# Output stores of the first ten token blocks issued from GpSimd's queue and not from SyncE's, in an attention and gated-FFN kernel

## Chip, cores and metric

The kernel runs on one core of one Trainium2 chip. The metric is the device time of one execution in microseconds (us); lower is better. The time of a version is the median of several executions.

The engines are called as the profile calls them: PE is TensorE (matrix products), PEld its weight loads, DVE is VectorE, ACT is ScalarE, POOL is GpSimd, SP is SyncE. SP computes nothing here; it issues DMAs. SPq and POOLq are the instruction queues of SP and POOL: an engine works its instructions off in order, so an instruction that waits holds up all that stand behind it on the same engine.

## The reference

Decayed linear attention over 4 batches, 8 heads, 768 positions and 64 channels, then a feed-forward network whose hidden layer is multiplied by its own cosine.

```python
for b in range(nb):                       # blocks of 64 positions
    intra = einsum('bhic,bhjc->bhij', qb, kb) * Dmask      # lam ** (i - j) below the diagonal
    intra = einsum('bhij,bhjd->bhid', intra, vb)
    inter = einsum('bhid,bhde->bhie', qb * lam_pow, kv_state)
    out[:, :, sl] = intra + inter
    kv_state = lam_block * kv_state + einsum('bhsd,bhse->bhde', kb * rev_pow, vb)
x = out.transpose(0, 2, 1, 3).reshape(3072, 512)
h = x @ w_in                              # 512 -> 2048
return (h * cos(h)) @ w_out               # 2048 -> 512, float32
```

## The kernel before

The 3072 tokens are 24 blocks of 128, numbered 0 to 23. Seven tiles of 4, 2, 3, 4, 4, 4 and 3 blocks (`TILES`) go through the feed-forward network one after the other. While the network works on one tile, attention is computed for the blocks of the next.

A block of attention takes these steps. SP loads its q, k and v rows from HBM (L221, three DMAs of 256 KB). POOL makes `qk` of them (q times a decay, L275; k cast to bf16, L279) and `v_s` (v times a decay, L283). Then q and k are transposed into `qkT`: for blocks 4 to 7 by PE (L301) with a copy by DVE (L304), from block 8 on by a DMA that SP issues (L307). PE computes the scores (L332), DVE masks them (L339), PE forms the values (L357, L361) and the state (L345), ACT writes the values as a column of `xT` (L367). Blocks 0 to 3 are handled earlier, in two spans of two blocks, with rows of even and odd number in the upper and the lower half of the partitions.

The network of a tile: `hidden` (L579, 16 slices of four products each), cosine by ACT (L586), the product by DVE (L592), then `project` (L624) for each block, 16 products in four chunks of four. ACT copies a finished block out of PSUM into `o_sb` (L636; three buffers), and a DMA stores it to `out`. Blocks 0 to 3 are stored by two DMAs each (L642), since their rows lie in halves: 64 rows of 2 KB, every other row of the output. All others are stored by one DMA (L644) of 128 rows. The last block goes in two pieces, by SP and ACT.

The order of the instructions on each engine is fixed ahead of time, by a planner in the kernel itself. Each step is a task with an engine, a cost in us, the tasks that it needs, and a priority. `Planner.order` keeps a clock for every engine and, again and again, places the task that can start first; among those of one engine that can start at the same time the lower priority number wins. The tasks are then emitted in the order of their planned starts. A DMA is two tasks: the issue, which takes time on the issuing engine's clock, and the transfer, on a single clock called DMA. A block's store becomes a task once its `project_out` is planned, so on its engine it stands behind whatever was planned to start before that copy's end, and ahead of all that was planned later. If on the chip that engine is ahead of its plan, the store waits for the copy, and what is behind it waits too.

POOL's queue holds, before the change: the building of constants, a part of the spans' preparation, the eight weight loads (L251, L254), and from 36 us on the preparation of blocks 4 to 23, three instructions each in the order q, k, v. SP's queue holds the loads, the transposes and the stores. A load of block n+2 is placed behind the transpose of block n.

The planner's call for a store, before the change, is the two lines

```python
eng, queue = ("DVE", "SP") if last and piece == 0 else ("ACT", "ACT" if last else "SP")
d = dma(queue, 0.7, 0.4, partial(store_out, queue), n0 + j + 8, [e], ordered=False)[1]
```

where 0.7 is the planned transfer and 0.4 the planned issue.

Of the kernel before, what the change touches and what calls it, by code (L numbers as in the profile page):

```python
# [12 lines left out]
AF = mybir.ActivationFunctionType  # L13
ALU = mybir.AluOpType

DMA_FROM = 8
QK = 4
THIRD = 1
# [82 lines left out]
def kernel(  # L101
# [10 lines left out]
    nc = tc.nc  # L112
    B, H, S, D = q.shape
    P = 128
# [18 lines left out]
    def bank(tag, shape, dt):  # L133
        return psum.tile(shape, dt, tag=tag, bufs=BUFS[tag], name=tag)
# [62 lines left out]
    live = {}  # L197
# [14 lines left out]
    def dma(queue, us, issue_us, emit, prio, deps=(), get=None, ordered=True):  # L212
        t = pl.add(queue, issue_us, list(deps) + [last_issue.get(queue) if ordered else None], emit, prio, get=get)
        if ordered:
            last_issue[queue] = t
        d = pl.add("DMA", us, [t], None, prio, lat=1.9)
        d.issue = t
        return t, d
# [47 lines left out]
    def add_attention(n):  # L266
# [42 lines left out]

        if n >= DMA_FROM:  # L310
            first_out, T[n] = dma("SP", 1.2, 1.3, transposes_dma, n - LAG + 1.5, [a, b], get="qkT", ordered=False)
# [250 lines left out]
    def add_ffn(i):  # L562
        nb, n0 = TILES[i], first[i]
        cols = nb * P
        gate = {}


        third = "ps_f" if i == 0 else "ps_t" if i >= THIRD else "ps_h"

        def bank_of(f):  # L570
            return third if f % 3 == 1 else "ps_h"

        for f in range(KF):
            pr = begins[i] + f * unit[i] / KF

            def hidden(f=f):
                t = bank(bank_of(f), [P, 4 * P], F32)
                for kd in range(KD):
                    ins = nc.tensor.matmul(t[:, :cols], lhsT=w_in_sb[:, kd, f * P:(f + 1) * P],  # L579
                                           rhs=live["xT", i][:, kd, :cols], start=(kd == 0), stop=(kd == KD - 1))  # L580
                live["h", i, f] = t
                return ins

            def cosine(f=f):
                c = work.tile([P, 4 * P], F32, tag="cos", name="cos")
                nc.scalar.activation(c[:, :cols], live["h", i, f][:, :cols], AF.Sin, bias=halfpi)  # L586
                live["c", i, f] = c

            def gated(f=f):
                if ("g", i) not in live:  # L590
                    live["g", i] = work.tile([P, KF, 4 * P], BF16, tag="g", name="g")
                nc.vector.tensor_mul(live["g", i][:, f, :cols], live.pop(("h", i, f))[:, :cols],  # L592
                                     live.pop(("c", i, f))[:, :cols])

            h = pl.add("PE", MM(cols, 4), [Vo[n] for n in range(n0, n0 + nb)] + [w_t["in", f * WCH // KF]],
                       hidden, pr, get=bank_of(f))
            a = pl.add("ACT", 0.26 + cols * 0.000833, [h], cosine, pr, get="cos")
            d = pl.add("DVE", 0.16 + cols * 0.00104, [a] + ([o_last[i - 2]] if i >= 2 else []), gated, pr)
            h.frees = [d]
            a.frees = [d]  # L600
            gate[f] = d
            h_last[i] = hid_t[i, f] = h
        nxt = unit[i + 1] if i + 1 < len(unit) else unit[i]
        U4 = 4
        for j in range(nb):
            last = n0 + j == NBLK - 1
            tag = ("ps_s", "ps_o", "ps_f", "ps_o")[(nb - 1 - j) % 4] if i == len(TILES) - 1 else "ps_f"
            if i == 0 and j == 1:
                tag = "ps_o"

            pieces = [slice(0, DM // 2), slice(DM // 2, DM)] if last else [slice(0, DM)]
            store = None
            for piece, part in enumerate(pieces):
                width = part.stop - part.start
                for f0 in range(0, KF, U4):
                    pr = begins[i + 1] + (j + f0 / KF) * nxt / nb + piece

                    def project(j=j, f0=f0, tag=tag, piece=piece, part=part, width=width):
                        if f0 == 0 and piece == 0:
                            live["f", i, j] = [bank("ps_s", [P, 2, DM], F32)[:, 0] if tag == "ps_s" else bank(tag, [P, DM], F32)]  # L620
                        elif f0 == 0:
                            live["f", i, j].append(bank("ps_t", [P, DM], F32))
                        for f in range(f0, f0 + U4):
                            nc.tensor.matmul(live["f", i, j][piece][:, :width], lhsT=live["g", i][:, f, j * P:(j + 1) * P],  # L624
                                             rhs=w_out_sb[:, f, part], start=(f == 0), stop=(f == KF - 1))

                    t = pl.add("PE", MM(width, U4), [gate[f] for f in range(f0, f0 + U4)] + [w_t["out", f0 * WCH // KF], store],
                               project, pr, get=None if f0 else "ps_t" if piece else tag)
                    if f0 == 0:
                        head = t  # L630
                    store = t
                o_last[i] = store

                def project_out(eng, j=j, i=i, piece=piece, width=width):
                    o = live["o_sb", i, j, piece] = work.tile([P, DM], F32, tag="o_sb", bufs=BUFS["o_sb"], name="o_sb")
                    (nc.scalar.copy if eng == "ACT" else nc.vector.tensor_copy)(o[:, :width], live["f", i, j][piece][:, :width])  # L636

                def store_out(eng, j=j, piece=piece, part=part, width=width):
                    r0 = (n0 + j) * P
                    if n0 + j < 2 * SPANS:  # L640
                        for s, h in enumerate(halves):
                            nc.sync.dma_start(out=out[r0 + s:r0 + P:2, :], in_=live["o_sb", i, j, piece][h])  # L642
                        return
                    (nc.scalar if eng == "ACT" else nc.sync).dma_start(  # L644
                        out=out[r0:r0 + P, part], in_=live["o_sb", i, j, piece][:, :width])

                eng, queue = ("DVE", "SP") if last and piece == 0 else ("ACT", "ACT" if last else "SP")
                e = pl.add(eng, 0.12 + width / 1060.0, [store], partial(project_out, eng), begins[i + 1] + (j + 1) * nxt / nb,
                           get="o_sb")
                d = dma(queue, 0.7, 0.4, partial(store_out, queue), n0 + j + 8, [e], ordered=False)[1]  # L650
                e.frees = [d]
                head.frees = [e]

# [19 lines left out]
    for i in range(len(TILES)):  # L673
        for n in range(max(2 * SPANS, first[i] + (i > 0)), min(first[i + 1] + 1, NBLK)):
            add_attention(n)
        add_ffn(i)
# [46 lines left out]
```

## Time and profile before

| | us |
|---|---|
| median of 5 runs | 217.64 (216.42 to 218.13) |
| the profiled execution | 216.02 |
| its span, first to last instruction | 214.3 |
| PE busy in the span | 205.7 (96%) |
| DVE busy | 120.0 (56%) |
| ACT busy | 108.3 (51%) |
| POOL busy | 66.3 (31%) |
| mean granted TensorE clock | 0.998 of full |

POOL's last computing instruction, the preparation of block 23, begins at 137.5 us; after it POOL is idle. SP's last load is issued at 124.5 us. Of the ten stores concerned the first is issued at 43.4 us and the tenth at 122.7 us. The DMA engines' mean busy share is given as 0.9 or more from about 5 to 125 us, and 0.1 to 0.2 afterwards except at the very end.

How to read the rows: a timeline line is start, duration, engine, line, operation and what it writes and reads; in square brackets the idle time ahead of it and what ended it. A line of the waits is engine and line, "<-" what it waited for, then the sum in us, the number of times and the longest. A line of the stretches is the stretch in us, its length, and then busy us (and instructions) of PE, PEld, DVE, ACT, POOL, the clock, the DMA engines' share and GB/s.

### The profile page before, as it was taken

How to read it: one execution, taken by the hardware profiler on the slowest of the kernel's cores; microseconds unless marked ns; L12 is line 12 of the kernel's file. 1: busy time of each engine (PE TensorE's matmuls, PEld its weight loads, DVE VectorE, ACT ScalarE, POOL GpSimd, SP SyncE). 2: the span in 40 equal slices, each digit the busy share in tenths (PEclk: the TensorE clock that was granted, in tenths of full speed). 3: DMA queues.
4: the chain of work that ended last, by engine and by line, in shares of the span. 5: the costliest groups of instructions: out<-in, count | busy, mean ns of one | idle time of the engine just before them, and what ended most of it. 6: DMA issues, size and time to landing. Idle time of an engine off the chain costs nothing.

```text
span 214.3 us, 4423 instructions
## 1 busy us (share of the span) xinstructions
PE 205.7 (96%) x1759; PEld 110.1 (51%) x1759; DVE 120.0 (56%) x212; ACT 108.3 (51%) x185; POOL 66.3 (31%) x85
## 2 busy tenths in 40 slices
PE   6799999999998999899999999999999999999994
PEld 6465444556764555445454444554545445555453
DVE  2693773455986787757656546746746434343300
ACT  5697873124755666443554544444444544445320
POOL 4594002867436554563546213400000000000000
PEclk9999999999999999999999999999999999999999
DMA  4999999999999999999999997221101101111112
GB/s 136 346 230 207 205 205 211 248 260 227 239 191 221 238 234 227 244 245 227 223 246 208 281 222 77 69 54 52 49 0 52 49 0 49 52 49 49 49 50 98
DMA packets 93588, 33.84 MB, mean 158 GB/s; under 512 B 80128, under 2 KB 90624, under 8 KB 93568
## 3 DMA queue, kind: packets, MB, share of 16 engines
q1 hardware_dynamic: 89200, 29.24, 59.3%
q0 software_dynamic: 4224, 4.19, 11.9%
q8 instruction: 13, 0.21, 0.4%
q10 hardware_dynamic: 144, 0.13, 0.2%
q14 instruction: 7, 0.06, 0.1%
HBM read 27.27 MB, written 6.29 MB: 157 GB/s over the span
## 4 chain that ended last, share of the span: by engine, by line
PE 82%; DMA 7%; ACT 3%; SPq 2%; POOL 1%; DVE 1%; issue 1%; ACTq 0%; POOLq 0%
PE ps_f L624 32%; PE ps_h L579 24%; PE ps_t L579 9%; DMA qkT<-qk 4%; PE ps_o L624 3%; PE ps_s L332 3%; PE ps_o L357 2%; PE ps_f L579 2%; PE ps_o L361 2%; DMA q_f<-in_q_dram 2%; PE ps_h L684 1%; DMA lam_bc<-in_lam_dram 1%; SPq L221 1%; ACT kv_bd L481 1%; SPq L307 1%; PE ps_t L624 1%
## 5 line engine op out<-in xcount | busy, mean ns | idle before, releaser
L624 PE MATMUL ps_f<-w_out_sb,g 128*128 128x512 bf16 x336 | 84.4, 379 | 0.2 <-ACT o_sb L636 0.2
L592 DVE TENSOR_TENSOR g<-ps_h,cos 128x512 bf16<-128x512 f32 (+2 forms) x77 | 47.2, 614 | 44.7 <-ACT cos L586 43.8
L586 ACT ACTIVATE cos<-ps_h,halfpi 128x512 f32<-128x512 f32 (+2 forms) x77 | 48.2, 626 | 47.3 <-PE ps_h L579 45.0
L579 PE MATMUL ps_h<-xT,w_in_sb 128*128 128x512 bf16 (+2 forms) x308 | 67.7, 349 | 0.2 <-ACT kv_bd L481 0.2
L579 PEld LDWEIGHTS <-w_in_sb 128*128 128x128 bf16 x448 | 43.3, 98 | 42.8 <-issue 1.2
L624 PEld LDWEIGHTS <-g 128*128 128x128 bf16 x400 | 37.7, 98 | 38.5 <-issue 0.3
L275 POOL TENSOR_TENSOR qk<-q_f,q_scale 128x512 bf16<-128x512 f32 x20 | 20.9, 1043 | 52.0 <-DMA q_f<-in_q_dram 31.1
L592 DVE TENSOR_TENSOR g<-ps_t,cos 128x512 bf16<-128x512 f32 (+2 forms) x30 | 18.0, 601 | 18.5 <-ACT cos L586 18.2
L339 DVE TENSOR_TENSOR s_m<-ps_s,mask 128x512 bf16<-128x512 f32 x40 | 26.0, 686 | 4.0 <-PE ps_s L332 3.6
L586 ACT ACTIVATE cos<-ps_t,halfpi 128x512 f32<-128x512 f32 (+2 forms) x30 | 18.5, 616 | 17.7 <-PE ps_t L579 16.5
L579 PE MATMUL ps_t<-xT,w_in_sb 128*128 128x512 bf16 (+2 forms) x120 | 26.5, 344 | 0.2 <-DVE g L592 0.2
L283 POOL TENSOR_TENSOR v_s<-v_f,v_scale 128x512 bf16<-128x512 f32 x20 | 20.9, 1043 | 11.0 <-DMA v_f<-in_v_dram 9.3
L636 ACT COPY o_sb<-ps_f 128x512 f32<-128x512 f32 x21 | 12.3, 586 | 16.5 <-PE ps_f L624 16.5
L367 ACT CAST xT<-ps_o 128x512 bf16<-128x512 f32 x20 | 11.6, 582 | 7.5 <-PE ps_o L361 7.4
L351 DVE CAST kv_bd<-ps_kv 64x256 bf16<-64x256 f32 x32 | 13.4, 417 | 2.8 <-PE ps_kv L345 2.4
L279 POOL CAST qk<-k_f 128x512 bf16<-128x512 f32 x20 | 12.2, 610 | 3.8 <-DMA k_f<-in_k_dram 3.6
L684 PE MATMUL ps_h<-blank,ident 128*128 128x128 bf16 (+1 forms) x59 | 9.0, 322 | 1.6 <-POOL ident masks.py:199 1.6
L332 PE MATMUL ps_s<-qkT 64*128 64x128 bf16 x160 | 7.9, 219 | 1.6 <-DMA qkT<-qk 1.6
L361 PE MATMUL ps_o<-s_m,v_s 128*64 128x128 bf16 x160 | 7.9, 220 | 0.0
L624 PE MATMUL ps_o<-w_out_sb,g 128*128 128x512 bf16 x32 | 7.7, 379 | 0.0
L357 PEld LDWEIGHTS <-kv_bd 128*64 128x64 bf16 x136 | 4.3, 109 | 6.7 <-issue 5.8
L357 PE MATMUL ps_o<-qkT,kv_bd 128*64 128x128 bf16 x136 | 7.0, 225 | 0.0
(88 smaller groups left out, 108.1 us busy)
## 6 DMA issues: line engine op xcount, KB each, us to landing
q_f<-in_q_dram SPq DMA_DIRECT2D x20, 256.0 KB, 3.7
k_f<-in_k_dram SPq DMA_DIRECT2D x20, 256.0 KB, 4.1
v_f<-in_v_dram SPq DMA_DIRECT2D x20, 256.0 KB, 4.3
out_dram<-o_sb SPq DMA_DIRECT2D x19, 256.0 KB, 2.1
w_in_sb<-in_moe_w_in_dram POOLq DMA_DIRECT2D x4, 512.0 KB, 8.1
w_out_sb<-in_moe_w_out_dram POOLq DMA_DIRECT2D x4, 512.0 KB, 14.2
out_dram<-o_sb SPq DMA_DIRECT2D x9, 128.0 KB, 2.5
q_f_sp<-in_q_dram SPq DMA_DIRECT2D x2, 512.0 KB, 5.2
```

Source lines behind the costliest of these rows:

```text
L275: (nc.vector if n == 0 else nc.gpsimd).tensor_mul(live["qk", n][:, 0], live.pop(("q_f", n)), q_scale[:, c, :].unsqueeze(2).to_broadcast([P ...
L279: (nc.scalar.copy if early else nc.gpsimd.tensor_copy)(live["qk", n][:, 1], live.pop(("k_f", n)))
L283: nc.gpsimd.tensor_mul(live["v_s", n], live.pop(("v_f", n)), v_scale[:, c, :].unsqueeze(2).to_broadcast([P, H, D]))
L332: nc.tensor.matmul(t[:, i, p, :], lhsT=live["qkT", n][h, 1, p, :], rhs=live["qkT", n][h, 0, p, :], start=True, stop=True)
L339: nc.vector.tensor_mul(live["s_m", n][:, i], live["s", n][:, i], mask.unsqueeze(1).to_broadcast([P, NP, P]))
L351: (nc.scalar.copy if early else nc.vector.tensor_copy)(kv_bd[n % NK][h, :, h], kv_ps[h])
L357: nc.tensor.matmul(t[h, p, :], lhsT=kv_bd[(n - 1) % NK][:, p, h], rhs=live["qkT", n][:, 0, p, :], start=(p == 0), stop=False, skip_group_c ...
L579: ins = nc.tensor.matmul(t[:, :cols], lhsT=w_in_sb[:, kd, f * P:(f + 1) * P], rhs=live["xT", i][:, kd, :cols], start=(kd == 0), stop=(kd = ...
L586: nc.scalar.activation(c[:, :cols], live["h", i, f][:, :cols], AF.Sin, bias=halfpi)
L592: nc.vector.tensor_mul(live["g", i][:, f, :cols], live.pop(("h", i, f))[:, :cols], live.pop(("c", i, f))[:, :cols])
L624: nc.tensor.matmul(live["f", i, j][piece][:, :width], lhsT=live["g", i][:, f, j * P:(j + 1) * P], rhs=w_out_sb[:, f, part], start=(f == 0) ...
L636: (nc.scalar.copy if eng == "ACT" else nc.vector.tensor_copy)(o[:, :width], live["f", i, j][piece][:, :width])
```

## The change

The stores of blocks 0 to 9 are issued by POOL; those of blocks 10 to 22 stay on SP, and the last block is as it was. In the planner a POOL store costs 1.0 for its issue where an SP store costs 0.4. Blocks 0 to 3 make two DMAs each, so 14 DMAs change their queue: eight of 128 KB and six of 256 KB.

```diff
+POOL_STORES = 10
...
                     if n0 + j < 2 * SPANS:
                         for s, h in enumerate(halves):
-                            nc.sync.dma_start(out=out[r0 + s:r0 + P:2, :], in_=live["o_sb", i, j, piece][h])
+                            nc.gpsimd.dma_start(out=out[r0 + s:r0 + P:2, :], in_=live["o_sb", i, j, piece][h])
                         return
-                    (nc.scalar if eng == "ACT" else nc.sync).dma_start(
+                    {"ACT": nc.scalar, "SP": nc.sync, "POOL": nc.gpsimd}[eng].dma_start(
                         out=out[r0:r0 + P, part], in_=live["o_sb", i, j, piece][:, :width])
 
-                eng, queue = ("DVE", "SP") if last and piece == 0 else ("ACT", "ACT" if last else "SP")
+                eng, queue = ("DVE", "SP") if last and piece == 0 else ("ACT", "ACT" if last else "POOL" if n0 + j < POOL_STORES else "SP")
...
-                d = dma(queue, 0.7, 0.4, partial(store_out, queue), n0 + j + 8, [e], ordered=False)[1]
+                d = dma(queue, 0.7, 1.0 if queue == "POOL" else 0.4, partial(store_out, queue), n0 + j + 8, [e], ordered=False)[1]
```

## The prediction

> **What bounds the kernel now.** I read the engines' shares first, then busy time by stretch, then what PE waits for, then the queues of SP and POOL around those waits.
>
> PE is the bound, busy for 205.7 of 214.3 us, and its work is the same before and after. So the change can only act through PE's stalls. By stretch (the first column of busy time is PE):
>
> ```profile
> 40.00:50.00 10.00, 9.77 (x113) 5.45 (x112) 5.38 (x10) 2.35 (x4) 7.22 (x10) 1.00 1.03 241
> 50.00:60.00 10.00, 9.81 (x105) 7.05 (x104) 7.84 (x19) 6.73 (x15) 5.23 (x6) 1.00 0.93 225
> 60.00:70.00 10.00, 9.30 (x104) 5.51 (x98) 7.40 (x16) 5.07 (x10) 5.34 (x6) 1.00 1.14 220
> 70.00:80.00 10.00, 10.00 (x111) 6.12 (x111) 8.54 (x17) 6.47 (x12) 5.33 (x6) 1.00 1.16 234
> 80.00:90.00 10.00, 9.61 (x108) 5.10 (x106) 7.17 (x13) 6.41 (x11) 5.34 (x6) 1.00 1.11 234
> 90.00:100.00 10.00, 9.50 (x78) 4.69 (x79) 6.64 (x13) 3.99 (x8) 5.28 (x6) 1.00 1.11 243
> ```
>
> Between 30 and 200 us PE lacks 0.23 + 0.19 + 0.70 + 0.39 + 0.50 = 2.0 us, all of it here; the other stretches show 10.00 of 10.00. What PE is without before 20 us and after 211 us lies outside the stores concerned. So 2.0 us is the most that this execution can gain. PE's timeline, and then the list of its waits, say what the stalls are:
>
> ```profile
> 65.22 0.40 PE L332 MATMUL ps_s<-qkT 64*128 64x128 bf16 x8 [0.69 <-DMA qkT<-qk]
> 90.50 0.40 PE L332 MATMUL ps_s<-qkT 64*128 64x128 bf16 x8 [0.90 <-DMA qkT<-qk]
> ```
>
> ```profile
> PE ps_f L624 <- ACT o_sb L636: 0.2, 1, 0.2
> PE ps_t L579 <- DVE g L592: 0.2, 1, 0.2
> ```
>
> 1.6 of the 2.0 us are the scores of block 9 and of block 14, waiting for the DMA transposes. SP's queue shows why these are late:
>
> ```profile
> 49.67 2.28 SPq L642 DMA_DIRECT2D out_dram<-o_sb  x2
> ...
> 53.44 2.85 SPq L642 DMA_DIRECT2D out_dram<-o_sb  x4
> 56.46 1.36 SPq L307 DMA_TRANSPOSE qkT<-qk  x1
> ...
> 60.30 2.87 SPq L307 DMA_TRANSPOSE qkT<-qk  x1
> ...
> 85.08 1.44 SPq L644 DMA_DIRECT2D out_dram<-o_sb  x1
> 86.63 1.31 SPq L307 DMA_TRANSPOSE qkT<-qk  x1
> ```
>
> SP issues without a gap here. POOL finished `qk` of block 8 at 51.98 (cast at 51.37, 0.61 long), but its transpose is issued at 56.46; `qk` of block 9 is done at 56.02, its transpose comes at 60.30; that of block 14 is done at 83.23, its transpose comes at 86.63, directly behind a store. The profile names POOL's later preparations as what SP waits for at the transposes. For block 8 it names one that begins with the transpose's issue and isn't needed for it, so I don't believe that name and go by the order of the queue.
>
> **Part 1: what SP gets rid of.** The 14 issues took, by their timeline rows, 1.50 + 2.28 + 2.85 for blocks 0 to 3, and 0.76, 1.44, 0.53, 1.15, 0.88, 0.53 for blocks 4 to 9: 11.9 us of SP. Ahead of the transposes of blocks 8 and 9 stand 6.6 us of them. Without these, block 9's transpose is limited by its data: even with POOL later (part 3) `qk` is ready near 58.2, and with the 4.88 us that the chain gives from issue to landing it lands at 63.1. PE arrives for it at 64.53 (65.22 less 0.69): stall gone, 0.69. For block 14, 1.44 us less ahead of it put the issue at 85.2; 3.83 us to landing make 89.0, and PE arrives at 89.60: stall gone, 0.90. Sum: -1.6 us, cover 1.4 and 0.6 us. The remaining 0.4 us have other causes and stay. Bounds: 0, if the DMA engines, whose share is 0.93 to 1.16 here, fill SP's freed time with longer issues; and -2.0, all stalls.
>
> [...]
>
> **Part 2: what one issue costs on POOL.** No store by POOL is in the trace. The nearest row is POOL's weight load, four in 2.97 us:
>
> ```profile
> 15.67 2.97 POOL L254 DMA_DIRECT2D w_out_sb<-in_moe_w_out_dram  x4
> 36.05 1.04 POOL L275 TENSOR_TENSOR qk<-q_f,q_scale 128x512 bf16<-128x512 f32 x1 [17.41 <-DMA q_f<-in_q_dram]
> 37.03 0.60 POOL L279 CAST qk<-k_f 128x512 bf16<-128x512 f32 x1
> 38.10 1.04 POOL L283 TENSOR_TENSOR v_s<-v_f,v_scale 128x512 bf16<-128x512 f32 x1 [0.46 <-DMA v_f<-in_v_dram]
> 39.10 1.04 POOL L275 TENSOR_TENSOR qk<-q_f,q_scale 128x512 bf16<-128x512 f32 x1
> ```
>
> That is 0.74 us each (0.80 for `w_in`), same engine, larger transfer. Below I bound it by SP's shortest store, 0.33; above by SP's longest half-block store, 1.64. I take 0.74, the row of the engine itself: 14 x 0.74 = 10.4 us of POOL, which is busy 31%.
>
> **Part 3: what stands behind the stores on POOL.** The preparations of blocks 4 to 9 are tight (36 to 57.5 us: 16 us of work, waits for loads between); later ones are not. Walk through it at 0.74, two issues for each of blocks 0 to 3:
> - Store 0 stands behind the k cast of block 4 (ends 37.63); its copy ended at 37.09, so no wait. 1.48 us: v of block 4 starts at 39.11, q of block 5 ends at 41.2 where it ended at 40.14. PE wanted it at 40.62: 0.6 late.
> - Store 1 stands behind the k cast of block 5 (41.8; copy done 40.99). Then v to 44.3, q and k of block 6 to 45.3 and 45.9; PE wants them at 45.66: about 0.1 late.
> - Store 2 stands behind the k cast of block 6 and waits for its copy, done at 46.45: here POOL runs ahead of its plan. To 47.93; v of block 6 to 49.0, q of block 7 to 50.0; PE wanted it at 49.22: 0.8 late.
> - Store 3 stands between q and k of block 9, copy long done (53.11). `qk` of block 9 near 58.2, as used above.
> - Stores 4 to 9: copies end at 67.21, 81.37, 94.22, 103.98, 114.0 and 121.92. POOL is idle for 1 to 7 us a block there, waiting for loads; the longest wait that I find, 1.3 us ahead of v of block 16, is needed by PE 9 us later. Nothing.
>
> With PE's order as it is, and block 7 met after PE is already 0.7 late, this sums to +1.5 us. But the planner is told of 1.0 a store, so the transposes of blocks 5 and 7 become due later by some tenths, and it gives PE whatever can start first. PE's neighbouring task is a projection chunk of four products, 0.86 us in the chain of waits. One such chunk ahead of each of the two covers 0.6 and 0.8. I take that this happens at both, which leaves +0.2 us. If the cover is missing at both it is the +1.5. The trace can't show which. At 0.33 an issue the same walk gives no lateness; at 1.64, in the old order, 2.4 + 1.5 + 2.0 = +5.9.
>
> **Sum.** -1.6 + 0.2 = -1.4 us on the profiled execution: 216.02 to 214.6, span 212.9. That execution was 1.6 us quicker than the median, so I put the same difference on the median: 217.64 - 1.4 = 216.2. The transfers themselves are the same bytes, earlier; 2.6 MB that come some 5 us sooner compete with loads that are needed sooner too, which I leave at nothing since what SP then loads is two blocks ahead.
>
> **Rivals.** What a measurement can tell from no change is about 0.5%, 1.1 us.
> - Given back on POOL: the stalls go, PE's order stays, +1.5 against -1.6: 217.5. For it: POOL is nearly full between 36 and 58 us with six us of issues more. Against: the due times do move. 20%.
> - POOL becomes the bound of blocks 5 to 7: an issue costs 1.2 us, between 0.74 and 1.64. The same walk in the old order: 1.64 late at block 5, 0.65 at block 6, 1.2 at block 7, +3.5 - 1.6 = +1.9: 219.5. It decides from about 1.0 us an issue (+2.7 - 1.6 = +1.1). For it: half-block stores on SP took up to 1.64 with the DMA engines full. Against: POOL's own rows are 0.74 to 0.84, with the DMA engines as full (share 1.17). 29%.
> - Hidden anyway: DMA engines are full to 125 us, so transposes come no earlier and both stalls stay; with +0.2 to +1.5 from POOL that is 217.8 to 219.1. [...] Against: the order alone puts block 9's transpose 4.3 us behind its data. 8%.
>
> **How the numbers follow.** The forecast, 216.2, has 43%. Faster by over 0.5%: 0.43. Within: 0.20 and none of the third rival's 0.08 but its lower end, together 0.22. Slower: 0.29 and the rest, 0.35. The forecast's own range is 215.6 (all 2.0 us) to 216.6. The whole range goes to 215.1 below, half a us under all stalls for the runs' scatter, and to 219.3 above, just short of the second rival's value, which leaves out about half of that rival.
>
> **What would show it.** Right: PE's waits for `qkT` gone at blocks 9 and 14; the transposes of blocks 8 and 9 issued near 54 and 58 us; POOL's store rows near 0.74 us; PE's transposes of blocks 5 and 7 each one chunk further back; stretches of 40 to 100 us short of full by 0.6 us and not 2.0. Wrong: PE waiting at L301 for `qk` or v (POOL late), POOL's store rows at 1 us and over, or the same waits for `qkT` with SP's issues grown longer.

## The result, and the profile after

Median of the changed kernel 217.56 us (216.85 to 218.84, 44 runs), of the kernel before 217.37 us (215.45 to 220.90, 79 runs). The ratio is 1.0025, 95% interval 1.0011 to 1.0038: slower by a quarter of a per cent, where 1.4 us less was forecast. The ratio leaves out executions over 1.5% above the fastest of their kernel: 13 of the 79, and none of the 44. The profiled execution took 217.66 us, its span 215.9, against 216.02 and 214.3 before.

Line numbers of the changed kernel are one higher (L625 for L624 and so on). First the busy time by stretch, changed kernel, columns as before (the first after the length is PE):

```profile
40.00:50.00 10.00, 9.77 (x110) 5.32 (x109) 5.37 (x10) 2.34 (x4) 8.10 (x12) 1.00 1.09 272
50.00:60.00 10.00, 9.16 (x94) 6.88 (x92) 7.34 (x17) 6.35 (x14) 7.72 (x10) 1.00 1.10 232
60.00:70.00 10.00, 10.00 (x112) 6.15 (x111) 8.08 (x18) 5.54 (x12) 5.83 (x7) 1.00 1.07 185
...
80.00:90.00 10.00, 9.38 (x82) 4.74 (x76) 6.14 (x11) 5.03 (x9) 5.81 (x8) 1.00 1.24 229
90.00:100.00 10.00, 10.00 (x102) 5.11 (x100) 7.96 (x15) 5.57 (x10) 5.54 (x7) 1.00 1.26 233
```

PE lacks 0.23 + 0.84 + 0.62 = 1.7 us here, where it lacked 2.0. So there is a gain of 0.3 us in the stretch that the prediction looked at, and the stalls are other ones. PE's timeline, changed kernel:

```profile
49.23 1.04 PE L625 MATMUL ps_f<-w_out_sb,g 128*128 128x512 bf16 x4
...
53.94 0.60 PE L580 MATMUL ps_h<-xT,w_in_sb 128*128 128x256 bf16 x4 [0.20 <-DVE g L593]
...
55.24 0.61 PE L302 MATMUL ps_t<-ident,qk 128*128 128x128 bf16 x8
...
59.58 0.60 PE L580 MATMUL ps_t<-xT,w_in_sb 128*128 128x256 bf16 x4 [0.64 <-DVE g L593]
...
86.33 0.40 PE L333 MATMUL ps_s<-qkT 64*128 64x128 bf16 x8 [0.62 <-DMA qkT<-qk]
```

The scores of blocks 9 and 14 wait no more. In their place come a wait of 0.64 us for DVE's product and one of 0.62 for the transpose of block 13. The transposes of block 7 (L302) stand at 55.24; before they began at 49.22.

POOL's stores in the changed kernel's timeline:

```profile
37.42 1.15 POOL L643 DMA_DIRECT2D out_dram<-o_sb  x2
...
41.29 1.09 POOL L643 DMA_DIRECT2D out_dram<-o_sb  x2
...
46.75 1.09 POOL L643 DMA_DIRECT2D out_dram<-o_sb  x2 [1.75 <-ACT o_sb L637]
...
53.35 1.09 POOL L643 DMA_DIRECT2D out_dram<-o_sb  x2 [0.89 <-ACT o_sb L637]
...
67.99 0.59 POOL L645 DMA_DIRECT2D out_dram<-o_sb  x1
```

An issue takes 0.56 us for a half block (median of eight) and 0.58 for a whole one (median of six).

So where did the time go? PE's last product begins at 210.53 us, before at 210.92: the changed kernel is still 0.4 us ahead there. The rest is at the very end, on ACT. The last pieces of the chain that ended last (start, duration, what), kernel before:

```profile
211.21 0.03 ACTq L636
211.24 0.04 issue
211.28 0.37 ACT o_sb L636
```

and the changed kernel:

```profile
210.82 0.03 ACTq L637
210.85 0.32 issue
211.17 0.37 ACT o_sb L637
```

"issue" is time in which ACT waits for nothing that the profile shows. It is 0.28 us longer. Then the last store, ACT's timeline, before:

```profile
211.28 0.37 ACT L636 COPY o_sb<-ps_t 128x256 f32<-128x256 f32 x1 [2.95 <-PE ps_t L624]
211.68 0.37 ACTq L644 DMA_DIRECT2D out_dram<-o_sb  x1
```

and after:

```profile
211.17 0.37 ACT L637 COPY o_sb<-ps_t 128x256 f32<-128x256 f32 x1 [3.23 <-PE ps_t L625]
211.57 1.76 ACTq L645 DMA_DIRECT2D out_dram<-o_sb  x1
```

The same instruction, 128 KB by ACT, takes 1.39 us longer to issue. The DMA queues in the stretch from 210 to 213 us (packets, MB, share) show what else is there in the changed kernel:

```profile
q1 hardware_dynamic: 153, 0.15, 14.8%
q14 instruction: 1, 0.01, 0.9%
```

One packet of 8 KB, kind "instruction", beginning at 211.8 us; the packets of ACT's store come only after 213. In the kernel before, the packet of that kind nearest the end begins at 206.2 us, when ACT waits for PE anyway (2.00 us, until 207.74). Its DMA queues from 205 to 207 us:

```profile
q1 hardware_dynamic: 73, 0.15, 19.8%
q14 instruction: 1, 0.01, 1.4%
```

Below such a packet is called a refill, and a row is one instruction of an engine in the trace. That it brings ACT its next instructions is the author's reading of the kind's name; the trace names no engine for it.

The account of the profiled executions: -0.39 to PE's end, +0.28 ahead of ACT's copy, +1.39 in ACT's store, and 0.35 behind it. The last is in SP's closing list of waits, some 0.06 us a row, where the entry for ACT's store was the last row and now has six more behind it. Sum +1.6, as the spans say. The 0.35 comes with the stores on POOL: after_one and queue_only (below) have it too, with 3.74 and 3.75 us from the start of PE's last product to the end, where the kernel before has 3.39.

### The profile page after: what moved, and what is told of

Its sections match the earlier page's. It is cut to its first block, busy times and chain, and to the rows that moved or that the text cites. A ratio compares the mean times of both kernels' runs of the same rounds, so it can differ in the third digit from the quotient of the medians.

```text
span 215.9 us, 4426 instructions
## 1 busy us (share of the span) xinstructions
PE 205.4 (95%) x1759; PEld 110.2 (51%) x1759; DVE 120.1 (56%) x212; ACT 108.2 (50%) x185; POOL 73.7 (34%) x99
## 4 chain that ended last, share of the span: by engine, by line
PE 81%; DMA 7%; ACT 4%; SPq 4%; POOL 1%; issue 1%; DVE 1%; ACTq 0%; POOLq 0%
PE ps_f L625 32%; PE ps_h L580 23%; PE ps_t L580 8%; PE ps_o L625 3%; DMA v_f<-in_v_dram 3%; DMA qkT<-qk 3%; PE ps_s L333 2%; PE ps_o L358 2%; PE ps_f L580 2%; SPq L308 2%; PE ps_o L362 2%; SPq L222 2%; PE ps_h L685 1%; DMA lam_bc<-in_lam_dram 1%; ACT kv_bd L482 1%
## 5 line engine op out<-in xcount | busy, mean ns | idle before, releaser
L625 PE MATMUL ps_f<-w_out_sb,g 128*128 128x512 bf16 x336 | 84.4, 379 | 0.2 <-ACT o_sb L637 0.2
L625 PEld LDWEIGHTS <-g 128*128 128x128 bf16 x400 | 37.8, 98 | 38.7 <-issue 0.3
L593 DVE TENSOR_TENSOR g<-ps_t,cos 128x512 bf16<-128x512 f32 (+2 forms) x30 | 18.0, 600 | 16.4 <-ACT cos L587 16.1
L625 PE MATMUL ps_o<-w_out_sb,g 128*128 128x512 bf16 x32 | 7.7, 379 | 0.0
```

## The experiments

Theory A: the middle is quicker, and the end is slower in every execution, because the place at which ACT's stream is refilled now falls on its last instructions. Theory B: that end is chance, and the time is lost among PE's stalls. Ratios are to the kernel before, run on the same chip.

**The changed kernel again** (after_again).

> The changed kernel once more, nothing else. In its first profile PE ends its last product 0.4 us earlier than in the profile of before (210.8 against 211.2), yet the span is 1.6 us longer: ACT's last copy begins 0.3 us after PE is done, not 0.05, and ACT's one store takes 1.76 us to issue, not 0.37, with a fetch of 8 KB on queue 14 (kind instruction) in that time. Theory A (ACT's instructions come late at the end, in every execution, since the place of the fetch in ACT's stream is fixed): the ACT store takes 1.5 us or more again, and the span is 215.2 to 216. Theory B (that tail is chance; the time goes to PE's stalls between 40 and 100 us): the ACT store takes 0.4 us, the span is near 214, or PE's stalls there are 3 us and not 1.7.

Ratio 0.999 (0.9959 to 1.0022), span 215.4. ACT's store took 1.93 us, with the 8 KB packet at 211.1. As A has it. On this chip PE's last product began at 209.83.

**The kernel before again** (before_again).

> The kernel before once more, for a second profile beside those of the changed one and as a null (ratio 1.000 within its interval). Theory A (the place of the last fetch in ACT's stream is fixed by the program): ACT's store issues in 0.4 us again and the 8 KB fetch on queue 14 comes 4 to 6 us ahead of it. Theory B (chance): it may come as late as in the changed kernel. Both: PE waits for qkT 1 to 3 us between 40 and 100 us.

Ratio 0.9971 (0.9934 to 1.0007): a null of the expected size. Its ACT store took 0.37 us, and the refill began 5.1 us ahead of ACT's last copy. PE waited 3.9 us for `qkT` in its profile (an execution of 220.60 us), where 1 to 3 were expected.

**The two parts alone.** queue_only issues the ten blocks' stores by POOL in the old plan; plan_only has the new plan and issues them by SP.

```diff
 # queue_only, on the kernel before
+POOL_STORES = 10
...
-                            nc.sync.dma_start(out=out[r0 + s:r0 + P:2, :], in_=live["o_sb", i, j, piece][h])
+                            nc.gpsimd.dma_start(out=out[r0 + s:r0 + P:2, :], in_=live["o_sb", i, j, piece][h])
...
-                    (nc.scalar if eng == "ACT" else nc.sync).dma_start(
+                    (nc.scalar if eng == "ACT" else nc.gpsimd if n0 + j < POOL_STORES else nc.sync).dma_start(
 # plan_only, on the changed kernel
-                            nc.gpsimd.dma_start(out=out[r0 + s:r0 + P:2, :], in_=live["o_sb", i, j, piece][h])
+                            nc.sync.dma_start(out=out[r0 + s:r0 + P:2, :], in_=live["o_sb", i, j, piece][h])
...
-                    {"ACT": nc.scalar, "SP": nc.sync, "POOL": nc.gpsimd}[eng].dma_start(
+                    {"ACT": nc.scalar, "SP": nc.sync, "POOL": nc.sync}[eng].dma_start(
```

> Stores of blocks 0 to 9 by POOL, but planned as before on SP at 0.4, so PE's order is that of before. My walk at the measured POOL issue (1.1 us for two halves): block 5's transposes 0.3 us late, block 7's 0.5 late, against 1.6 us of stalls gone at blocks 9 and 14: PE ends 0.5 to 1.0 us earlier than before. Theory A: what the time does with that hangs on ACT's tail (store issue 0.4 or 1.8). Theory B (PE's new order costs the time): 0.3 to 0.6% faster than before.

> The new plan (a store costs 1.0 on POOL's clock), but all stores issued by SP. PE's order is that of the changed kernel. Theory A: the new order alone moves PE's end by under 1 us: the waits for DVE's products near 53 and 59 us (0.84) come in, and the transposes' lateness of before (1.6) stays or moves; ACT's tail as in the changed kernel if it hangs on the order of ACT's stream: 0.3 to 1% slower than before. Theory B: slower by 0.3% or more with ACT's store at 0.4 us.

queue_only: 0.9964 (0.9923 to 1.0005), ACT's store 0.37 us. plan_only: 1.0019 (0.9985 to 1.0054), ACT's store 1.76 us. Neither ratio can be told from 1; the store's time can: the late end goes with the new plan and not with the queue. That left two readings: the plan's order as such, or the length of ACT's stream, which is 326 rows in the traces of before and of queue_only, and 325 in those of the changed kernel and of plan_only (one wait fewer that needs a row of its own).

**Sixteen tiny copies** (after_pad, after_pad2, before_pad2). Two 128x1 copies on ACT behind the output copies of blocks 10 to 17, where ACT is half idle (busy 24.07 of 50 us from 150 to 200 us in the kernel before). after_pad writes them to a new tile, the other two to `warm`, which exists.

```diff
                     (nc.scalar.copy if eng == "ACT" else nc.vector.tensor_copy)(o[:, :width], live["f", i, j][piece][:, :width])
+                    for _ in range(2 if 10 <= n0 + j < 18 else 0):
+                        nc.scalar.copy(warm, halfpi)
```

> The changed kernel with 16 tiny ACT copies (128x1, two behind each output copy of blocks 10 to 17, where ACT is idle half of the time), so that ACT's stream is some 20 instructions longer ahead of its end. Theory A: the last fetch of ACT's instructions now falls 16 or more instructions before the end, at a place where ACT waits for PE; the ACT store issues in 0.4 us, the span is 1.2 to 1.7 us shorter, ratio to the kernel before 0.994 to 0.998. Theory B: the ratio stays at 1.002 to 1.004.

1.0050 (1.0023 to 1.0076). ACT's store was back at 0.37 us, as A has it, but the kernel was slower; PE's wait at the start for DVE's `q_sp` was 1.3 us and its waits for `qkT` 1.5, against 0.8 and 0.6 in the changed kernel's profile. Hence the next two.

> The changed kernel with the 16 tiny ACT copies again, now written to a tile that is there anyway. In the first padded kernel ACT's store did issue in 0.37 us, but the whole kernel was 1.3 us slower, with later waits at the very start; it had a new tile of 4 bytes that moved all that were allocated after it. Theory A: without that tile 1.2 to 1.7 us quicker than the changed kernel, ratio to before 0.992 to 0.997. Theory A2 (the copies themselves, or their place, cost what the tail gains): ratio 1.000 to 1.005 again. Theory B: no change of the tail.

> The kernel before with the same 16 copies: the control. Theory A: its last fetch already falls ahead of the end, so there is nothing to gain: ratio 1.000, within 0.3%. Theory A2: slower by 0.3 to 0.6%.

after_pad2: 0.9875 (0.984 to 0.991), median 215.97 us. before_pad2: 0.9975 (0.994 to 1.0011). Both issue ACT's store in 0.37 us. The same copies gain 1% and more on the changed kernel and nothing that can be told on the kernel before.

**One tiny copy** (after_one): the loop above, once, behind block 10.

> The changed kernel with a single tiny ACT copy (128x1), behind the output copy of block 10. In the changed kernel's trace the late fetch starts 1 us after ACT's queue takes up its last copy; one row more ahead of it should move that point to the wait ahead of the last copy, some 3.4 us earlier, where ACT is idle. Theory A (the place of the fetch alone): as with 16 copies, store issue 0.4 us, 1.2 to 1.7 us quicker than the changed kernel. Rival A2 (the 16 copies helped in another way, say by pacing ACT in the later tiles): one copy does nothing, store issue 1.8 us.

0.9906 (0.9872 to 0.994), median 216.18 us. One row is enough. ACT's timeline at the end:

```profile
210.49 0.37 ACT L637 COPY o_sb<-ps_t 128x256 f32<-128x256 f32 x1 [2.95 <-PE ps_t L625]
210.89 0.37 ACTq L647 DMA_DIRECT2D out_dram<-o_sb  x1
```

and its DMA queues from 205 to 207 us, where the refill now is:

```profile
q1 hardware_dynamic: 144, 0.26, 34.7%
q14 instruction: 1, 0.01, 1.6%
```

So the gain doesn't need sixteen copies that pace ACT in some other way. On the same chip the changed kernel took 218.38 us (after_again): 2.2 us more, of which its end explains 0.28 ahead of ACT's copy and 1.56 in ACT's store.

**The last store by SP** (after_last_sp, before_last_sp): no row added, but nothing of weight left on ACT behind the refill.

```diff
-                eng, queue = ("DVE", "SP") if last and piece == 0 else ("ACT", "ACT" if last else "POOL" if n0 + j < POOL_STORES else "SP")
+                eng, queue = ("DVE", "SP") if last and piece == 0 else ("ACT", "SP" if last else "POOL" if n0 + j < POOL_STORES else "SP")
```

> The changed kernel with the very last half-block stored by SP and not by ACT; no copies added. Theory A: ACT's fetch still comes at the end, but only the copy (0.3 us) and no DMA issue is behind it: 1.0 to 1.5 us quicker than the changed kernel, ratio to before 0.993 to 0.997. Theory B: unchanged, 0.999 to 1.003.

> The kernel before with the very last half-block stored by SP: the control to the changed kernel with the same edit. Theory A: its ACT store issued in 0.4 us anyway, so SP does it no quicker: ratio 1.000 within 0.4%. Rival: storing by SP is quicker for its own reasons: 0.993 to 0.996.

after_last_sp: 0.9897 (0.9857 to 0.9936), median 216.20. before_last_sp: 1.0033 (0.9993 to 1.0073). The edit helps only where the refill is late.

All three mended forms gained more than theory A gave for them (0.992 to 0.997, or 1.2 to 1.7 us). A reckoned with the end; PE's waits for `qkT`, compared further below, point to the middle for the rest.

**The two parts again, with the last store by SP** (plan_only_last_sp, queue_only_last_sp).

> The new plan with all stores issued by SP, the last one too, so the tail is out of the comparison. What PE's new order does by itself: waits for DVE's products (0.84 us against 0.19) come in, the transposes stay behind SP's stores. If the new order costs: 0.2 to 0.5% slower than before. If the order is what helps: 0.3% or more faster. With its ACT store at 1.8 us this kernel was at 1.002.

> The stores by POOL in the old plan, the last one by SP. What the queue does by itself: if it is the whole gain, 0.6 to 1.2% faster than before, like the changed kernel with its tail mended; if PE's transposes wait for POOL (0.9 us in the first look) or the gain needs the new order too, 0.2 to 0.5% faster.

0.9978 (0.9945 to 1.001) and 0.9982 (0.9944 to 1.0021). Neither part alone can be told from the kernel before; both together, on another chip, were 0.9897. The profiles say what each leaves: with the queue alone PE waits 0.68 us at block 7's transposes for POOL and 1.7 to 2.0 us for a `qkT`; with the plan alone the transposes stay behind SP's stores, and PE's waits for `qkT` were 2.2 and 0.6 us in its two profiles. Why the queue alone has the long wait at block 14 wasn't followed.

**The converse** (before_dve16, before_dve16_pad): the kernel before, block 16's output copy done by DVE, which takes two rows out of ACT's stream; and the same with two tiny copies that put them back.

```diff
-                    (nc.scalar.copy if eng == "ACT" else nc.vector.tensor_copy)(o[:, :width], live["f", i, j][piece][:, :width])
+                    (nc.scalar.copy if eng == "ACT" and n0 + j != 16 else nc.vector.tensor_copy)(o[:, :width], live["f", i, j][piece][:, :width])
 # before_dve16_pad
+                    for _ in range(1 if n0 + j in (10, 11) else 0):
+                        nc.scalar.copy(warm, halfpi)
```

> The converse test: the kernel before, with the output copy of block 16 (near 160 us, far from the end) done by DVE and not by ACT. That takes two rows out of ACT's stream (322 rows by counting instructions and the waits that need a row of their own, to 320; the changed kernel has 321). Theory A (the place of the fetch): the 8 KB fetch now falls on the end, the ACT store takes 1.5 us or more, and the kernel is 1.2 to 1.7 us slower than before: ratio 1.005 to 1.008. Rival A3 (late fetches belong to the new plan, however many rows): store at 0.4 us, ratio 1.000 within 0.3%.

> The same with two tiny ACT copies (behind the output copies of blocks 10 and 11), which bring ACT's stream back to 322 rows while DVE keeps the copy of block 16. Theory A: store at 0.4 us, ratio 1.000 within 0.3%. If it is DVE's copy that costs: slow like the kernel without the two copies.

before_dve16: 1.0098 (1.0068 to 1.0128). before_dve16_pad: 1.0038 (1.0005 to 1.007). ACT's timeline at the end, without the two copies:

```profile
213.50 0.37 ACT L636 COPY o_sb<-ps_t 128x256 f32<-128x256 f32 x1 [2.95 <-PE ps_t L624]
213.90 2.18 ACTq L644 DMA_DIRECT2D out_dram<-o_sb  x1
```

and with them:

```profile
213.98 0.37 ACT L636 COPY o_sb<-ps_t 128x256 f32<-128x256 f32 x1 [2.95 <-PE ps_t L624]
214.38 0.37 ACTq L646 DMA_DIRECT2D out_dram<-o_sb  x1
```

The kernel before gets the late end too, in its own plan, when its stream is shortened. The control isn't quite at 1.000: in both PE waits 0.4 us for DVE's copy. The difference of the two, 0.6%, is 1.3 us, of the order of the 1.8 us that the store took longer.

**A new tile of 4 bytes** (after_one_tile): after_one, writing to a new tile allocated ahead of the state tiles, as in after_pad.

> The changed kernel with one tiny ACT copy, which was 0.991, but writing to a new tile of 4 bytes ahead of all the state tiles, as in the first padded kernel that was 1.005. If the shift of the tiles was what spoiled that one: ratio 1.000 or more, later waits at the very start. If that kernel was slow by the place of its 16 copies or by chance: 0.988 to 0.994.

1.0057 (1.0027 to 1.0088), against 0.9906. So the tile is what spoiled after_pad; ACT's store was at 0.37 us in both. DMA issues (KB each, median us to landing), after_one:

```profile
k_f_sp<-in_k_dram SPq DMA_DIRECT2D x2, 512.0 KB, 5.6
v_f_sp<-in_v_dram SPq DMA_DIRECT2D x2, 512.0 KB, 6.0
```

and after_one_tile:

```profile
k_f_sp<-in_k_dram SPq DMA_DIRECT2D x2, 512.0 KB, 6.5
v_f_sp<-in_v_dram SPq DMA_DIRECT2D x2, 512.0 KB, 7.3
```

The first loads of k and v take 0.9 and 1.3 us longer to land. That the tiles allocated behind the new one move is the author's reading of the program; the traces give no addresses.

The ends of the kernels in which ACT issues the last store, in one table (rows of ACT in the trace; that store; the start of the last refill on queue 14, in us behind the start of ACT's last copy, minus for ahead of it):

| kernel | ACT rows | ACT store, us | last refill, us |
|---|---|---|---|
| before; queue_only | 326 | 0.37 | -5.0; -5.1 |
| before, again | 326 | 0.37 | -5.1 |
| changed; plan_only | 325 | 1.76 | +0.7 |
| changed, again | 325 | 1.93 | +0.7 |
| after_one; after_one_tile | 326 | 0.37 | -5.1 |
| after_pad | 341 | 0.37 | -16.2 |
| after_pad2; before_pad2 | 341; 342 | 0.37 | -16.1; -16.7 |
| before_dve16 | 324 | 2.18 | +1.0 |
| before_dve16_pad | 326 | 0.37 | -5.1 |

The versions that beat both kernels are after_pad2, after_last_sp and after_one, at 216.0 to 216.2 us, each with the kernel before at 218.5 to 218.9 on its chip.

## Why the prediction was wrong

The step that failed is in "What bounds the kernel now": "What PE is without before 20 us and after 211 us lies outside the stores concerned." The stores lie outside, but the change doesn't end with them. It put the plan's tasks in another order, this took one row out of ACT's stream, and the refill moved from 206.2 us, where ACT waits for PE, to 211.8 us, onto the last store. That cost 0.28 + 1.39 us, and no term of the sum stood for it; nor for the 0.35 us behind it that the stores on POOL add to SP's closing waits, which after_one still pays. With one row put back, the kernel is at 216.18 us; the number forecast was 216.2.

That agreement is luck: on that chip the kernel before took 218.52 us, and the middle went otherwise than forecast, point by point:
- Part 1, SP's relief: right in kind. The transposes of blocks 8 and 9 are issued at 55.10 and 59.01, forecast near 54 and 58, and both named stalls (0.69 and 0.90) are gone. But block 13's transpose, issued at 80.25, landed only as PE had waited 0.62 us. It took 6.04 us from issue to landing, where 3.83 and 4.88 had been taken for blocks 14 and 9 from the trace of before. The sum left it "at nothing" that the earlier transfers compete with others. The DMA engines' share there is 1.24, before 1.11, but that this is the reason isn't shown. The -1.6 was -1.0 in this execution.
- The size differs from execution to execution, which the prediction saw only in the spread of the runs. PE's waits for `qkT` were 1.3 to 3.3 us in five profiles of the kernel before and its variants with all stores on SP in the old plan (3.9 in that of before_again), and 0 to 0.6 us in five of the changed kernel and its mended forms with the tiles in place. So the gain was 2.0 to 2.7 us by the ratios on the two chips where mended forms ran.
- Part 2, the price of an issue: mis-sized, 0.56 and 0.58 us where 0.74 was taken; 14 of them took 8.0 us and not 10.4.
- Part 3, POOL: the wait of store 2 for its copy came (1.75 us idle), another at store 3 (0.89 us) was not seen: it stands between q and k of block 8, not of block 9, and POOL comes to it earlier than reckoned. So `qk` of block 8 is done only at 55.07, and its transpose is issued at 55.10. PE waited for neither.
- PE's order: block 5's transposes moved behind one chunk, as taken. Block 7's moved by 6.0 us, behind three chunks and seven slices of `hidden`. That covers POOL's lateness, and its price is new: the slices stand so close that PE overtakes ACT and DVE, 0.65 us more. In the old order PE waits for POOL, 0.68 us at block 7 (queue_only); that the gain needs the new order isn't shown, since most of what queue_only loses is its long wait at block 14.

Of the rivals, "given back on POOL" had the time (217.5) and not the cause: it was given back at the end, by ACT. POOL as the bound and transposes as late as before didn't come.

## What to carry to other kernels

When an edit changes the order or number of instructions on an engine, as this one did on ACT, compare the last few us of each engine's queue before and after, and look for packets of kind "instruction" there: this edit at 40 to 120 us cost 1.7 us at 211. In these runs a refill that fell where ACT waits anyway left its last store at 0.37 us, and one row more (0.9906), or the last store on another queue (0.9897), was worth more than the edit itself (1.0025). And a small step that improves a stretch can be judged only after the ends of the two kernels have been made alike.

## What the runs showed of the hardware

- In the changed kernel's span the packets of kind "instruction" are 7 of 8 KB on queue 14 and 14 of 16 KB on queue 8. The traces don't name their engines. The last one of 8 KB goes with ACT's stream: one row more there, with the rows of the other issuing engines unchanged, moves it from 211.8 to 205.4 us. Whose those of 16 KB are isn't shown. Where the last one of 8 KB began 0.7 to 1.0 us behind the start of ACT's last copy, ACT's store took 1.76 to 2.18 us; where it began 5.0 us or more ahead of it, the store took 0.37 us.
- In two executions with a long wait of PE the granted clock was lower. In queue_only_last_sp PE waited 2.0 us for a `qkT`, until 92.0 us; in the stretch around it (columns as above, the clock is the third number from the end) it was granted 0.72 on average:

```profile
89.00:90.00 1.00, 1.00 (x26) 0.65 (x24) 0.82 (x2) 0.82 (x2) 0.35 (x1) 1.00 0.54 121
90.00:95.00 5.00, 2.71 (x22) 1.14 (x16) 2.73 (x5) 0.61 (x2) 2.58 (x3) 0.72 1.03 191
```

  Four products of `hidden` took 1.79 us from 94.13 us, and 1.03 from 96.62. From 60 to 100 us the mean clock was 0.96 in this profile and 0.96 in that of before_again, where PE's longest wait was 2.3 us; in queue_only, where it was 1.7 us, the clock was 1.00. What length of wait lowers the clock isn't shown by these three profiles, nor that it is the wait that does.
- after_one_tile differs from after_one by a new tile of 4 bytes, and was 1.5% slower (1.0057 against 0.9906), with the first loads of k and v landing 0.9 and 1.3 us later. The reason isn't shown.
